# Attention and a two-layer network on one core: part of the early pooling on GpSimd, and seven products in a sixth chunk's second layer

## The chip, the cores and the metric

The kernel runs on one core of one Trainium2 chip. The core has five engines that the program feeds: TensorE (PE; its weight loads are shown apart as PEld), VectorE (DVE), ScalarE (ACT), GpSimd (POOL) and SyncE (SP, which here only starts transfers), and 16 DMA engines. Each engine takes its instructions in the order in which the program gives them and waits at the first one that isn't ready. The metric is the device time of one execution in microseconds (us); of several runs the median is given.

## The reference, cut to what matters

```python
# q, k, v: (8, 8, 576, 64)      moe_x is the attention's output as (8, 576, 512)
k_p = k.reshape(B, H, 72, 8, D).mean(axis=3)         # keys and values pooled by 8
v_p = v.reshape(B, H, 72, 8, D).mean(axis=3)
scores = (1/8) * q @ k_p.T;  scores -= max(scores)
attn = exp(scores) / (sum(exp(scores)) + 1e-9)
x = attn @ v_p                                       # 4608 tokens of 512
xn = (x - mean(x)) / sqrt(var(x) + 1e-6) * g_ln
out = x + maximum(xn @ w_ch1, 0) @ w_ch2             # 512 -> 2048 -> 512
```

## The kernel before, in words

**Numbers.** Results have to be good to float32, while TensorE is fed 16-bit numbers. So each large factor is kept as a high part and a low part, both float16, and each product is three matmuls (high by high, high by low, low by high). Wherever a factor is made, two steps make it: one rounds to the high part (mostly on ScalarE), one subtracts to get the low part (VectorE or GpSimd).

**Tiles and chunks.** The 4608 tokens are 36 tiles of 128; four tiles make a chunk of 512 (nine chunks, 0 to 8). For each batch of 576 tokens the keys and values are pooled first. `load_k`/`pool_k` (L622 to L630) load four pairs of heads of 128x72x8 numbers; a reduce on VectorE (L627) sums the innermost eight, and two copies (L630) put the halves on the diagonal blocks of `kblk`. `load_v`/`pool_v` (L634 to L640) do it for each of eight heads (72x64x8), with one reduce into `vp` (L640). When a batch's `vp` is whole, `max_v` takes its largest value (L644) and `all_max` spreads it over the partitions with a small matmul (L447), after which `split_v` makes the scaled high and low parts `vh`, `vb`, and a DMA lays `vh` out as `va` for the matmuls. Batch 0's values and keys are pooled by functions of their own.

`stage_a` of a tile is scores, maximum and exponentials (matmuls L754); `stage_b` is the values (matmuls L886, L887), the division, the mean and variance, and the normalized `z` with its two parts. Where a tile holds tokens of two batches, L893 copies two batches' scales into `cvm`. From chunk 3 on, L935 makes the normalization's bias from mean and scale (`ln`), one number for each of 128 tokens, for ScalarE.

**The network.** Chunks 0 and 1 have plain products in layer 1 (`ffn_in`, matmuls L1070); from chunk 2 on layer 1 is done as a 2x2 scheme with seven products in place of eight (`product`, L1114). In layer 2, chunks 0 to 3 have plain products (`ffn_out`, matmuls L1265: eight groups of 24 matmuls of 512 columns for a chunk, each group with one accumulation into `x`, L1276). Chunks 4 to 8 have seven products (`out_seven`, L1231: 336 matmuls of 256 columns for a chunk, with 28 groups of 12). `C_TWO = 4` is the first of these. Plain and seven-product chunks prepare the hidden activations differently: `whole_h` (ScalarE L1140, VectorE L1144) for the plain ones; for seven products `left_factors`, `right_relu`, `right_sums` and `right_pair`: a rounding on ScalarE and the low part (L1152) on VectorE or GpSimd, with four sums on GpSimd in between (L1169, L1170, L1172, L1173). `right_pair` with i = 1 always takes its low part on GpSimd, with i = 0 only for chunks in `LO_GPSIMD`. Seven products also need seven factors of w2. Four of them are sums that `sums_w2` makes once (tokens TW; VectorE, GpSimd, ScalarE) and writes to DRAM (`w2s`); three are copies (KW); each chunk loads its factors again, in 14 transfers of 512 KB (`load_w2`, L1220), into four buffers that lie in the place of `ring`.

**The order.** Two tables, START and STEADY, set the order of all work. A token names a function and its arguments; each time it stands in the table, that function runs on by one step (to its next `yield`), so that the tables interleave matmuls, splits, loads and prepared batches. All engines' queues, the DMA queue of SP among them, follow from this one order. START reaches up to the first `product`; the weights w1 and w2 are also loaded, taken to float32 (`convert`, tokens C, L520) and split in it (`split`, tokens S: L460 or L462 the high part on ScalarE, L467 the low part on VectorE, or L464 on GpSimd for the four blocks of w2's first half that `LO_POOL` names; the first second-layer matmuls, tokens G.0, need them), so that it holds work for VectorE, ScalarE and GpSimd that later stretches don't.

Of the kernel before, what the change touches and what calls it, by code (L numbers as in the profile page):

```python
# [31 lines left out]
C_TWO = 4  # L32
# [33 lines left out]
R.2.1 R.2.1 A.3 D.0 D.0 R.2.2 R.2.2 A.3 M1.0 B.1 A.3 A.3 E.3.0 M1.0 M1.0 S.1.0 E.3.0 B.1 B.1 B.0 B.0 B.0 E.2.0 E.2.0
E.2.1 E.2.1 B.2 E.3.1 B.1 C.2.0 S.1.0 S.1.0 S.1.1 C.2.0 C.2.0 C.1.3 C.1.3 C.1.2 C.1.2 S.1.1 S.1.1 B.2 B.2 B.0 B.0 B.1
S.1.2 E.3.1 B.2 E.3.0 E.3.0 S.1.2 S.1.2 S.1.3 C.2.2 C.2.1 E.3.1 E.3.1 B.3 HK.1.1 HK.1.1 R.2.3 R.2.3 A.4 R.1.4 R.1.4 B.1
B.1 HK.1.1 HK.1.1 A.4 A.5 S.1.3 S.1.3 F.0.0.0 F.0.1.0 F.0.0.0 B.2 F.0.1.0 A.4 A.5 F.0.2.0 A.4 F.0.2.0 C.2.2 HV.1.0
HV.1.0 F.0.0.0 F.0.0.0 F.0.3.0 F.0.3.0 C.2.3 F.0.1.0 F.0.1.0 F.0.4.0 F.0.4.0 C.2.2 C.2.2 C.2.1 C.2.1 C.2.1 HV.1.0  # L70
# [287 lines left out]
def attn_ffn_kernel(ctx: ExitStack, tc: tile.TileContext, qT, kT, v, kvn, kvt, g, w1, w2, out):  # L358
# [264 lines left out]

    def pool_k(b, p):
        kr = kraw.pop((b, p))
        kp = kr.rearrange("p k l -> p (k l)")[:, 0:KV]
        nc.vector.tensor_reduce(out=kp, in_=kr, axis=AX.X, op=ALU.add)  # L627
        for j in range(2):
            r, c = slice(j * D, (j + 1) * D), slice(j * KV, (j + 1) * KV)
# [776 lines left out]
```

## Time and profile before

| | us |
|---|---|
| median of 3 runs | 821.44 (820.87 to 822.48) |
| the profiled execution: its own time | 825.36 |
| its span | 823.6 |
| mean granted TensorE clock | 0.990 |

| busy in the span | us | share | instructions |
|---|---|---|---|
| PE | 788.5 | 96% | 6462 |
| DVE | 655.3 | 80% | 1328 |
| ACT | 453.5 | 55% | 848 |
| POOL | 441.4 | 54% | 521 |

The span is from the first to the last event of the profiled execution; 1.8 us of its time lie around it. A view by windows gives the busy time of each engine in each stretch, with the number of instructions, the granted clock of TensorE (1.00 is full speed), and the share of the 16 DMA engines' time. A view of waits says for how long an engine stood and which event ended it. Rows of a group of instructions have the line, the engine, the operation, out and in, the shape, the count, then the busy time in us, the mean of one in ns, and the idle time of the engine just before them with what ended it. The chain of waits is followed back from the last instruction.

### The profile page before, as it was taken

Reading aid. Unit: us, or ns where it says so; the run is one execution under the profiler, and the core shown is the slowest. Engines: PE = TensorE matmul, PEld = TensorE weight load, DVE = VectorE, ACT = ScalarE, POOL = GpSimd, SP = SyncE. Lnnn points to the kernel's source line nnn. Section 1 sums busy time; section 2 is a strip of 40 time slices with the busy share of each in tenths; the row PEclk is TensorE's granted clock in tenths of the full one; section 3 lists DMA queues with packets and bytes.
Section 4 is the critical chain, followed back from the end, with each engine's and each line's share of the span. In section 5 each row is a group of like instructions: output and inputs, shape, how many; then the busy total and the mean of one; then the engine's idle time right before and its main releaser. Section 6 shows DMA issues by size and latency. Waiting matters only on the chain.

```text
span 823.6 us, 16934 instructions
## 1 busy us (share of the span) xinstructions
PE 788.5 (96%) x6462; PEld 595.7 (72%) x6462; DVE 655.3 (80%) x1328; ACT 453.5 (55%) x848; POOL 441.4 (54%) x521
## 2 busy tenths in 40 slices
PE   6988999899999999999999999999999999999997
PEld 3876445444448765775668899889988889988886
DVE  5998999689586989789868988889788768765653
ACT  3988794141315635454448374856575737655461
POOL 0535335345261515763437574577488757785473
PEclk9989999899999999999999999999999999999999
DMA  9949746631045777666537469686756663654224
GB/s 359 333 125 254 215 126 141 150 90 27 1 106 146 168 157 185 164 158 153 134 105 205 155 190 221 152 243 137 214 146 156 174 178 99 166 166 142 90 104 153
DMA packets 179201, 131.54 MB, mean 160 GB/s; under 512 B 143536, under 2 KB 150832, under 8 KB 176944
## 3 DMA queue, kind: packets, MB, share of 16 engines
q1 hardware_dynamic: 177968, 129.57, 58.3%
q10 hardware_dynamic: 1152, 0.90, 0.5%
q8 instruction: 50, 0.82, 0.4%
q14 instruction: 31, 0.25, 0.1%
HBM read 81.79 MB, written 16.78 MB: 120 GB/s over the span
## 4 chain that ended last, share of the span: by engine, by line
PE 75%; DVE 16%; DMA 2%; ACT 2%; POOL 2%; issue 2%; ACTq 1%; DVEq 0%; POOLq 0%
PE ps_f L1114 29%; PE ps_f L1231 19%; PE ps_f L1265 13%; PE ps_f L1070 7%; PE ps_a L754 4%; DVE w L520 2%; DVE w L467 1%; PE ps_a L886 1%; DVE x L1248 1%; PE ps_m L694 1%; PE ps_a L887 1%; DMA vr<-in_v_dram 1%; DVE x L1276 1%; DVE raw L595 1%; DVE wm L504 1%
## 5 line engine op out<-in xcount | busy, mean ns | idle before, releaser
L1114 PE MATMUL ps_f<-zts,w 128*128 128x256 f16 x1680 | 207.2, 273 | 0.9 <-DVE x L1276 0.8
L1231 PE MATMUL ps_f<-ring,w 128*128 128x256 f16 x1680 | 193.7, 273 | 3.8 <-DVE x L1248 2.8
L1231 PEld LDWEIGHTS <-w 128*128 128x128 f16 x1680 | 163.7, 98 | 24.4 <-issue 4.0
L1114 PEld LDWEIGHTS <-w 128*128 128x128 f16 x1680 | 163.4, 98 | 22.1 <-issue 1.5
L1265 PE MATMUL ps_f<-w,ring 128*128 128x512 f16 x768 | 170.0, 379 | 1.5 <-DVE ring L1144 1.4
L1265 PEld LDWEIGHTS <-ring 128*128 128x128 f16 x768 | 74.2, 98 | 88.9 <-DVE ring L1144 3.6
L1133 ACT COPY raw<-ps_f 128x256 f32<-128x256 f32 x168 | 59.1, 372 | 94.3 <-PE ps_f L1114 87.5
L1152 POOL TENSOR_TENSOR w<-w 128x512 f16<-128x512 f32 x64 | 75.1, 1177 | 35.7 <-ACT w L1150 28.4
L1114 PE MATMUL ps_f<-zts,tsp 128*128 128x256 f16 x672 | 91.1, 273 | 0.8 <-ACT raw L1133 0.8
L1070 PE MATMUL ps_f<-zts,w 128*128 128x512 f16 (+1 forms) x480 | 88.4, 343 | 2.5 <-DVE x L1276 1.6
L790 POOL TENSOR_TENSOR phl<-e,phl 128x512 f16<-128x512 f32 x32 | 38.6, 1206 | 73.2 <-ACT phl L780 73.1
L1070 PEld LDWEIGHTS <-w 128*128 128x128 f16 x480 | 47.2, 99 | 40.4 <-issue 6.8
L1150 ACT CAST w<-w 128x512 f16<-128x512 f32 x80 | 48.9, 619 | 46.0 <-POOL w L1170 17.9
L1114 PEld LDWEIGHTS <-tsp 128*128 128x128 f16 x672 | 65.2, 98 | 9.4 <-issue 1.1
L1039 POOL TENSOR_TENSOR hl<-raw,hl 128x640 f16<-128x640 f32 x28 | 40.3, 1444 | 31.6 <-ACT hl L1037 23.2
L1248 DVE SCALAR_TENSOR_TENSOR x<-ps_f,y,x 128x256 f32<-128x256 f32 (+1 forms) x70 | 35.4, 518 | 26.2 <-PE ps_f L1231 25.6
L1248 DVE SCALAR_TENSOR_TENSOR x<-ps_f,cy,x 128x256 f32<-128x256 f32 (+1 forms) x70 | 35.2, 516 | 17.3 <-PE ps_f L1231 16.8
L1128 DVE TENSOR_TENSOR raw<-ps_f,raw 128x256 f32<-128x256 f32 x84 | 34.0, 416 | 18.5 <-PE ps_f L1114 9.6
L754 PE MATMUL ps_a<-kblk,q 128*128 128x144 f32 (+1 forms) x320 | 41.9, 289 | 1.7 <-issue 1.2
L754 PEld LDWEIGHTS ps_a<-kblk,q 128*128 128x128 f32 (+1 forms) x320 | 37.0, 179 | 4.9 <-issue 2.4
L1039 POOL TENSOR_TENSOR hl<-z,hl 128x512 f16<-128x512 f32 x18 | 23.9, 1327 | 30.8 <-ACT hl L1037 16.5
L1079 ACT ACTIVATE ring<-ps_f 128x512 f16<-128x512 f32 (+1 forms) x40 | 19.5, 508 | 37.9 <-PE ps_f L1070 33.3
(175 smaller groups left out, 1416.0 us busy)
## 6 DMA issues: line engine op xcount, KB each, us to landing
ring<-w2s SPq DMA_DIRECT2D x70, 512.0 KB
q<-in_qT_dram SPq DMA_DIRECT2D x36, 256.0 KB
out_dram<-x SPq DMA_DIRECT2D x36, 256.0 KB
tsp<-in_w_dram SPq DMA_DIRECT2D x8, 1024.0 KB
kr<-in_kT_dram SPq DMA_DIRECT2D x28, 288.0 KB
vr<-in_v_dram SPq DMA_DIRECT2D x56, 144.0 KB
raw<-in_w_dram SPq DMA_DIRECT2D x6, 1024.0 KB
w2s<-phl SPq DMA_DIRECT2D x32, 128.0 KB
```

The source lines that it names most:

```text
L754: nc.tensor.matmul(ps[r, p // 2, p % 2 * 2 * KV : (p % 2 + 1) * 2 * KV], lhsT=q[:, p, r], rhs=kblk[b % NKB][:, p, :], start=True, stop=True,)
L790: nc.gpsimd.tensor_tensor(out=ph[:, 0, :, KA:P], in0=e[:, :, 0:KA], in1=ph[:, 0, :, 0:KA], op=ALU.subtract)
L1039: nc.gpsimd.tensor_tensor(out=zhl[:, 1, :], in0=src, in1=zhl[:, 0, :], op=ALU.subtract)
L1070: nc.tensor.matmul(ps, lhsT=w[:, part, fs], rhs=zT[:, kz, cols], start=(n == 0), stop=(n == 3 * NKT - 1),)
L1114: nc.tensor.matmul(ps, lhsT=w[:, part, f * P : (f + 1) * P], rhs=z, start=m in (1, 2, 4, 5) and n == 0, stop=m in (2, 3, 4, 7) and n == 3 ...
L1128: nc.vector.tensor_tensor(out=o, in0=ps, in1=o, op=ALU.add)
L1133: nc.scalar.copy(out=o, in_=ps)
L1150: nc.scalar.copy(out=hi, in_=src)
L1152: engine.tensor_tensor(out=lo, in0=src, in1=hi, op=ALU.subtract)
L1231: nc.tensor.matmul(ps, lhsT=wt[2][:, left, part, f * HC + u * P : f * HC + (u + 1) * P], rhs=b[:, f // FPB, wp, f % FPB], start=n < 4 and ...
L1248: nc.vector.scalar_tensor_tensor(out=x, in0=ps, scalar=scale, in1=x, op0=ALU.mult, op1=ALU.add)
L1265: nc.tensor.matmul(ps, lhsT=h[:, part, i, cols], rhs=w[:, wp, j], start=(n == 0), stop=(n == 3 * NFT // 2 - 1),)
```

## The change

- `C_TWO` is 3, and STEADY has chunk 3's second layer as seven products (`out_seven` with its four preparing functions and its 14 loads) in place of eight groups of plain products and `whole_h`.
- `V_GPSIMD = (1, 2)`: the values of batches 1 and 2 (16 heads) are pooled by GpSimd, in three additions that halve each time (72x256, 72x128, 72x64), from a host layout in which the eight tokens of a group are not innermost. `K_GPSIMD = (2,)`: the same for the four key pairs of batch 2 (128x288, 128x144, then two additions of 64x72 that write straight to `kblk` and take the place of the two copies).
- `LO_GPSIMD` is empty: the low parts of `right_pair` with i = 0 in chunks 6, 7 and 8 (24 subtractions of 128x512) go from GpSimd to VectorE.
- The copies of L893 (eight of 64x3) go from VectorE to ScalarE. The bias of L935 (24 of 128x1) is written as a `tensor_scalar` with two scalars in place of a `scalar_tensor_tensor`. The place of `z` is taken one step later.
- START and STEADY are new tables: nearly all tokens stand elsewhere.

The counts that differ, by the kind of instruction (lines of the kernel before; left before, right with the change):

| engine, work | before | changed |
|---|---|---|
| PE L1265, matmul of 512 columns | 768 | 576 |
| PE L1231, matmul of 256 columns | 1680 | 2016 |
| DVE L640, reduce of one head's values | 56 | 40 |
| DVE L627, reduce of one pair's keys | 28 | 24 |
| DVE L630, copy into `kblk` | 56 | 48 |
| DVE L1144 / ACT L1140 | 32 | 16 |
| DVE L1276 | 32 | 24 |
| DVE L1248 (128x256 / 128x512) | 120 / 20 | 144 / 24 |
| DVE L1152, low part of 256 / of 512 from `raw`, `phl` | 40 / 40 | 48 / 48 |
| L1152, low part of 512 from `w`: DVE / POOL | 16 / 64 | 48 / 48 |
| POOL L1169, L1170, L1172, L1173, each | 40 | 48 |
| POOL, additions for pooling | 0 | 64 |
| SP, loads of 512 KB from `w2s` | 70 | 84 |

Three places show what the new order moves. In the changed program the line numbers are larger: L464 is L483 there, L790 and L793 are L823 and L826, L520 is L539, L640 and the new additions are L670 to L673, L1081 is L1114, L894 to L915 are L927 to L948, L1210 is L1243, L1220 is L1253.

GpSimd's queue around the four low parts of w2's first half (L464, `w` of 128x1024), before:

```order
L789 MEMSET phl_116 128x8x40
L790 TENSOR_TENSOR phl_116<-e,phl_116 128x8x64
L793 TENSOR_TENSOR phl_116<-e,phl_116 128x8x8
L464 TENSOR_TENSOR w_91<-w_91 128x1024
L790 TENSOR_TENSOR phl_115<-e,phl_115 128x8x64
L793 TENSOR_TENSOR phl_115<-e,phl_115 128x8x8
L719 MEMSET vh 72x8
L720 MEMSET vb 72x8
L464 TENSOR_TENSOR w_91<-w_91 128x1024 x3
L926 COPY ln<-cvm 128x2
```

and now:

```order
L483 TENSOR_TENSOR w_91<-w_91 128x1024
L647 TENSOR_TENSOR kr<-kr 128x288
L648 TENSOR_TENSOR kr<-kr 128x144
L655 TENSOR_TENSOR kblk_113<-kr 64x72 x2
L483 TENSOR_TENSOR w_91<-w_91 128x1024
L823 TENSOR_TENSOR phl_115<-e,phl_115 128x8x64
L826 TENSOR_TENSOR phl_115<-e,phl_115 128x8x8
L483 TENSOR_TENSOR w_91<-w_91 128x1024
L671 TENSOR_TENSOR vr<-vr 72x256
L672 TENSOR_TENSOR vr<-vr 72x128
L673 TENSOR_TENSOR vp<-vr 72x64
L483 TENSOR_TENSOR w_91<-w_91 128x1024
```

Before, three of the four stand in a row, with two attention tiles' low parts (`phl`) ahead. Now a pair of keys (L647 to L655) stands between the first and the second and a head of values (L671 to L673) ahead of the fourth; the eight heads of batch 1 stand further ahead in the queue.

VectorE's queue where w2 is taken to float32 (L520 before, L539 now), layer 1 of chunk 0 is taken out of PSUM (L1081 before, L1114 now) and a tile's values are finished, before:

```order
L640 TENSOR_REDUCE vp<-vr 72x64
L1081 SCALAR_TENSOR_TENSOR ring<-ps_f,ring 128x256 x2
L520 SCALAR_TENSOR_TENSOR w_91<-w_91,raw 128x1024
L640 TENSOR_REDUCE vp<-vr 72x64
L1081 SCALAR_TENSOR_TENSOR ring<-ps_f,ring 128x256
L894 TENSOR_SCALAR sm<-ps_a,cv 128x8
L902 RECIPROCAL rs<-sm 128x8
L904 TENSOR_TENSOR x<-ps_a,rs 128x512
L914 BN_STATS st<-x 128x6
L915 BN_AGGR ln<-st 128x2
L1081 SCALAR_TENSOR_TENSOR ring<-ps_f,ring 128x256 x2
L640 TENSOR_REDUCE vp<-vr 72x64
```

and now:

```order
L1114 SCALAR_TENSOR_TENSOR ring<-ps_f,ring 128x256
L539 SCALAR_TENSOR_TENSOR w_91<-w_91,tsp_92 128x1024
L539 SCALAR_TENSOR_TENSOR w_91<-w_91,tsp_93 128x1024
L927 TENSOR_SCALAR sm<-ps_a,cv 128x8
L935 RECIPROCAL rs<-sm 128x8
L937 TENSOR_TENSOR x<-ps_a,rs 128x512
L947 BN_STATS st<-x 128x6
L948 BN_AGGR ln<-st 128x2
L1114 SCALAR_TENSOR_TENSOR ring<-ps_f,ring 128x256 x2
L797 TENSOR_REDUCE mx<-ps_a 128x8
L802 TENSOR_TENSOR e<-ps_a,mx 128x576
L1114 SCALAR_TENSOR_TENSOR ring<-ps_f,ring 128x256
```

The reduces of single heads (L640) that stood between these are gone from VectorE's queue; two steps of w2 stand next to each other and the next tile's maximum and exponent step (L797, L802) follows sooner.

SP's queue around the first load of a w2 factor for the seven products (`ring<-w2s`), with the last writes of the sums to `w2s` ahead of it, before:

```order
L1210 DMA w2s_122<-phl_116 128x4x128 x2
L1281 DMA out_dram<-x 128x512
L634 DMA vr<-in_v_dram 72x512
L622 DMA kr<-in_kT_dram 128x576
L1281 DMA out_dram<-x 128x512
L634 DMA vr<-in_v_dram 72x512
L1220 DMA ring<-w2s_121 128x2048
L746 DMA q<-in_qT_dram 128x512
L634 DMA vr<-in_v_dram 72x512
L1281 DMA out_dram<-x 128x512
L801 DMA_TRANSPOSE pt<-phl_115 128x16x128
L1220 DMA ring<-w2s_121 128x2048
```

and now:

```order
L1243 DMA w2s_122<-phl_116 128x4x128 x4
L1314 DMA out_dram<-x 128x512
L661 DMA vr<-in_v_dram 72x512
L641 DMA kr<-in_kT_dram 128x576
L1243 DMA w2s_122<-phl_116 128x4x128 x2
L1253 DMA ring<-w2s_121 128x2048
L779 DMA q<-in_qT_dram 128x512
L661 DMA vr<-in_v_dram 72x512
L1253 DMA ring<-w2s_121 128x2048
L1314 DMA out_dram<-x 128x512
L834 DMA_TRANSPOSE pt<-phl_115 128x16x128
L661 DMA vr<-in_v_dram 72x512
```

Before, the first of these loads is the 178th row of SP's queue and comes for chunk 4; now it is the 152nd and comes for chunk 3, close behind the last write of the sums.

The diff, without the tables' rows:

```diff
-C_TWO = 4
+C_TWO = 3
...
-LO_GPSIMD = (6,7,8)
+K_GPSIMD, V_GPSIMD = (2,), (1, 2)
+LO_GPSIMD = ()
 START = """
-LN.2 LN.2 LK.0 LK.0 LK.1 LK.1 Q.0 Q.0 HK.1.0 R.1.0 R.1.0 V0 V0 K0 K0 K0 HK.1.0 HK.1.0 Q.1 Q.1 R.1.1 R.1.1 R.1.2 R.1.2
...
+LN.2 LN.2 LK.0 LK.0 LK.1 LK.1 Q.0 Q.0 R.1.0 R.1.0 R.1.1 R.1.1 Q.1 Q.1 R.1.2 R.1.2 R.1.3 R.1.3 A.0 HV.1.0 LG LG R.2.0
...
 def pool_k(b, p):
         kr = kraw.pop((b, p))
-        kp = kr.rearrange("p k l -> p (k l)")[:, 0:KV]
-        nc.vector.tensor_reduce(out=kp, in_=kr, axis=AX.X, op=ALU.add)
+        if b in K_GPSIMD:
+            kr = kr.rearrange("p k l -> p (k l)").rearrange("p (l k) -> p l k", k=KV)
+            nc.gpsimd.tensor_add(out=kr[:, 0:4, :], in0=kr[:, 0:4, :], in1=kr[:, 4:8, :])
+            nc.gpsimd.tensor_add(out=kr[:, 0:2, :], in0=kr[:, 0:2, :], in1=kr[:, 2:4, :])
+        else:
+            kp = kr.rearrange("p k l -> p (k l)")[:, 0:KV]
+            nc.vector.tensor_reduce(out=kp, in_=kr, axis=AX.X, op=ALU.add)
         for j in range(2):
...
-            nc.vector.tensor_copy(out=kblk[b % NKB][r, p, c], in_=kp[r])
+            if b in K_GPSIMD:
+                nc.gpsimd.tensor_add(out=kblk[b % NKB][r, p, c], in0=kr[r, 0, :], in1=kr[r, 1, :])
+            else:
+                nc.vector.tensor_copy(out=kblk[b % NKB][r, p, c], in_=kp[r])
...
-        nc.vector.tensor_reduce(out=vp[b][:, h, :], in_=vr, axis=AX.X, op=ALU.add)
+        if b not in V_GPSIMD:
+            nc.vector.tensor_reduce(out=vp[b][:, h, :], in_=vr, axis=AX.X, op=ALU.add)
+            return
+        vr = vr.rearrange("p d l -> p (d l)").rearrange("p (l d) -> p l d", d=D)
+        nc.gpsimd.tensor_add(out=vr[:, 0:4, :], in0=vr[:, 0:4, :], in1=vr[:, 4:8, :])
+        nc.gpsimd.tensor_add(out=vr[:, 0:2, :], in0=vr[:, 0:2, :], in1=vr[:, 2:4, :])
+        nc.gpsimd.tensor_add(out=vp[b][:, h, :], in0=vr[:, 0, :], in1=vr[:, 1, :])
...
-                nc.vector.tensor_copy(out=cv[r], in_=CV[b][r])
+                nc.scalar.copy(out=cv[r], in_=CV[b][r])
...
         if c > 2:
-            nc.vector.scalar_tensor_tensor(
-                out=ln[:, 0:1], in0=ln[:, 0:1], scalar=-1.0, in1=ln[:, 2:3], op0=ALU.mult, op1=ALU.mult
+            nc.vector.tensor_scalar(
+                out=ln[:, 0:1], in0=ln[:, 0:1], scalar1=ln[:, 2:3], scalar2=-1.0, op0=ALU.mult, op1=ALU.mult
             )
...
```

More of the change, by code (lines that the diff above doesn't have):

```diff
@@ L66 @@
[L66 to L70, printed above, removed]
@@ L101 @@
+F.1.15 F.1.15 V.10 HV.3.1 F.1.13 F.1.13 F.1.14 F.1.14 F.1.15 F.1.15 G.1.0.1 G.1.1.1 G.1.2.1 HK.3.1 HK.3.1 B.8 B.8 V.10
+U.1.1 U.1.0 V.10 V.10 HV.3.1 V.10 V.10 X X U.1.0 U.1.0 B.11 B.11 G.1.0.1 G.1.3.1 G.1.1.1 B.11 B.11 HV.3.1 HV.3.1 B.11
+B.11 B.11 G.1.0.1 G.1.0.1 HK.3.1 HK.3.1 U.0.0 U.0.0 U.1.1 U.1.1 G.1.2.1 G.1.2.1 G.1.2.1 G.1.1.1 G.1.1.1 G.1.3.1 G.1.3.1
+G.1.3.1
 """
 STEADY = """
-P.2.0.1.2 P.2.0.0.2 P.2.0.0.5 P.2.0.1.1 P.2.0.1.5 P.2.0.0.1 P.2.0.1.1 P.2.0.1.1 HV.4.0 A.12 A.12 A.13 TW.0.0.0 TW.0.0.0
@@ new lines @@
+P.4.1.0.7 A.22 P.4.1.0.5 P.4.1.0.5 P.4.1.0.3 P.4.0.3.3 P.4.0.3.3 EL.4.0.3 P.4.1.0.4 P.4.1.0.4 P.4.0.3.4 P.4.0.3.4
+EP.4.0.1.1 EP.4.0.1.0 EP.4.0.1.0 B.21 A.23 A.22 EL.4.0.3 EL.4.0.3 O.4.0.1.1 ES.4.0.2 EP.4.0.2.0 P.4.0.3.7 P.4.0.3.7
+O.4.0.1.0 ER.4.0.3 P.4.1.0.7 P.4.1.0.7 P.4.1.1.5 P.4.1.1.1 EP.4.0.1.1 EP.4.0.1.1 P.4.1.0.3 P.4.1.0.3 O.4.0.0.1
+O.4.0.0.0 EP.4.0.2.0 EP.4.0.2.0 ER.4.0.3 ER.4.0.3 ES.4.0.2 ES.4.0.2 B.20 B.20 EP.4.0.2.1 HV.6.1 HV.6.1 A.22 A.22
+LW.4.0.3 LW.4.0.3 ER.4.0.2 ER.4.0.2 P.4.1.1.5 P.4.1.1.5 EL.4.1.0 B.20 P.4.1.1.3 ES.4.0.3 EP.4.0.3.0 A.23 B.22 A.23
@@ new lines @@
+HV.6.1 HV.6.1 P.4.1.2.5 P.4.1.2.5 O.4.0.5.0 O.4.0.5.0 P.4.1.3.2 P.4.1.2.6 P.4.1.3.6 P.4.1.3.5 P.4.1.2.3 B.23 P.4.1.3.6
+P.4.1.3.6 P.4.1.2.6 P.4.1.2.6 P.4.1.3.5 P.4.1.3.5 B.22 B.22 P.4.1.2.2 P.4.1.2.2 P.4.1.2.4 P.4.1.3.7 P.4.1.3.3
+EP.4.1.0.1 EP.4.1.0.1 P.4.1.3.2 P.4.1.3.2 P.4.1.3.4 P.4.1.2.7 ES.4.1.1 ES.4.1.1 EP.4.1.1.1 Z.22.0 HV.6.1 P.4.1.2.3
+P.4.1.2.3 EL.4.1.2 P.4.1.2.4 P.4.1.2.4 Z.22.1 P.4.1.3.4 P.4.1.3.4 EP.4.1.1.0 EP.4.1.1.0 Z.22.0 Z.22.0 B.23 A.24
+EL.4.1.2 EL.4.1.2 Z.22.1 Z.22.1 P.4.1.3.3 P.4.1.3.3 EL.4.1.3 P.4.1.3.7 P.4.1.3.7 P.4.1.2.7 P.4.1.2.7 ER.4.1.2
@@ L353 @@
+O.8.1.5.0 O.8.1.5.1 O.8.1.5.1 O.8.1.5.1
 """
@@ L916, in values @@
         seven = c >= 2
-        if seven and tt >= 2:
-            if "z" not in t_raw:
-                t_raw["z"] = t_raw["b"].rearrange("p n c -> p (n c)")
-            z = t_raw["z"][:, :DM]
-        else:
+        Z[t] = ln
+        if not (seven and tt >= 2):
             z = wk1.tile([P, DM], F32, name="z")
-        Z[t] = ln
         if not seven:
@@ L933, in values @@
             yield
+            if tt >= 2:
+                if "z" not in t_raw:
+                    t_raw["z"] = t_raw["b"].rearrange("p n c -> p (n c)")
+                z = t_raw["z"][:, :DM]
         if c > 2:
-            nc.vector.scalar_tensor_tensor(
-                out=ln[:, 0:1], in0=ln[:, 0:1], scalar=-1.0, in1=ln[:, 2:3], op0=ALU.mult, op1=ALU.mult
+            nc.vector.tensor_scalar(
+                out=ln[:, 0:1], in0=ln[:, 0:1], scalar1=ln[:, 2:3], scalar2=-1.0, op0=ALU.mult, op1=ALU.mult
             )
@@ L1386 @@
         "qT": q.transpose(1, 3, 0, 2).reshape(NPAIR, P, NTT, P).transpose(2, 1, 0, 3),
-        "kT": k.reshape(B, NPAIR, 2, KV, POOL, D).transpose(0, 2, 5, 1, 3, 4).reshape(B, P, NPAIR, KV, POOL),
-        "v": v.reshape(B, H, KV, POOL, D).transpose(0, 2, 1, 4, 3),
+        "kT": np.stack([
+            k[i].reshape(NPAIR, 2, KV, POOL, D).transpose((1, 4, 0, 3, 2) if i in K_GPSIMD else (1, 4, 0, 2, 3)).reshape(P, NPAIR, KV, POOL)
+            for i in range(B)
+        ]),
+        "v": np.stack([
+            v[i].reshape(H, KV, POOL, D).transpose((1, 0, 2, 3) if i in V_GPSIMD else (1, 0, 3, 2)).reshape(KV, H, D, POOL)
+            for i in range(B)
+        ]),
         "kvn": np.stack([x[i].transpose(1, 0, 2).reshape(S, DM)[: S // P * P].reshape(S // P, P, DM).transpose(1, 0, 2) for x, i in ((k, 1), (v, 1), (v, 0))]),
```

573 lines of the change are left out of this document (291 added, 282 removed).

## The prediction, made before the changed kernel was run

> **What bounds the kernel now.** I read first the busy time of the engines, then the windows, then TensorE's waits in the windows where it stands, then the groups of those windows. The sum is made against the profiled execution: 825.36 us, of which the span is 823.6 and 1.8 lie around it. It is 3.9 above the median of the runs (821.44); the change is worked out in the span and then taken off the median.
>
> ```profile
> span 823.6 us, 16934 instructions
> PE 788.5 (96%) x6462; PEld 595.7 (72%) x6462; DVE 655.3 (80%) x1328; ACT 453.5 (55%) x848; POOL 441.4 (54%) x521
> ```
>
> TensorE works for 96% of the span and is idle for 35.1 us. So there are two ways to be faster: less work for TensorE, or fewer of these 35 us. The windows (start and end, length, then the busy time of each engine) show where they lie:
>
> ```profile
> core 0: us, PE busy (x) PEld busy (x) DVE busy (x) ACT busy (x) POOL busy (x), PEclk, DMA share, GB/s
> 0.00:20.60 20.60, 13.48 (x61) 7.72 (x61) 11.93 (x30) 6.34 (x8) 2.03 (x12) 1.00 0.92 359
> 20.60:103.00 82.40, 72.30 (x633) 55.25 (x634) 76.75 (x153) 69.65 (x98) 36.24 (x34) 0.96 0.76 232
> 103.00:144.10 41.10, 41.06 (x228) 20.74 (x226) 39.94 (x68) 29.07 (x41) 17.91 (x14) 1.00 0.54 133
> 144.10:164.70 20.60, 18.02 (x98) 8.32 (x97) 14.23 (x35) 3.25 (x5) 6.23 (x12) 0.83 0.69 150
> 164.70:245.90 81.20, 78.74 (x380) 35.80 (x379) 65.27 (x106) 21.79 (x38) 39.50 (x39) 1.00 0.22 55
> 245.90:448.00 202.10, 199.48 (x1589) 141.36 (x1589) 167.78 (x369) 105.10 (x214) 95.10 (x136) 1.00 0.64 154
> 448.00:597.00 149.00, 146.64 (x1399) 131.51 (x1398) 127.26 (x270) 90.00 (x181) 89.88 (x105) 1.00 0.73 191
> 597.00:803.00 206.00, 203.80 (x1950) 181.80 (x1948) 145.22 (x290) 126.14 (x263) 146.81 (x165) 1.00 0.51 142
> ```
>
> From 245.9, where START ends, TensorE is busy for 99% of each window up to 803: a matmul removed there comes off the end, as long as no other engine becomes late. START, in contrast, leaves 7.1 + 10.1 + 0.0 + 2.6 + 2.5 = 22.3 us idle, and VectorE is busy for 93% and 97% of the windows from 20.6 to 144.1. What ended TensorE's longest waits in START (total, times, longest):
>
> ```profile
> PE ps_m L694 <- DMA w<-in_kvn_dram: 6.2, 1, 6.2
> PE ps_m L835 <- ACT w L460: 4.5, 1, 4.5
> PE ps_m L447 <- DVE rowmax L425: 3.7, 2, 2.0
> PE ps_a L886 <- DMA va<-vh: 2.6, 1, 2.6
> ```
>
> The first is the first load, the second ScalarE. The third is a spread of a maximum that VectorE, late in its queue, hadn't given, and the fourth the layout `va` of a batch's values, a transfer behind eight heads' pooling and the maximum. Only the last two hang on the pooling.
>
> **The change part by part. 1: chunk 3's second layer.** Two pieces of the chain of waits (start, duration, work) hold unbroken matmuls of both kinds:
>
> ```profile
> 224.33 20.73 PE ps_f L1265 x96
> 799.63 18.36 PE ps_f L1231 x168
> ```
>
> A matmul of 512 columns takes 20.73/96 = 0.2159 us, one of 256 columns 18.36/168 = 0.1093. 192 of the first (41.45) go and 336 of the second (36.72) come: **-4.7 us** of TensorE's work. The order shows exactly these counts, so this term is the surest; it needs the preparation (part 3) to be in time.
>
> **2: the pooling.** What leaves VectorE, and what GpSimd has that is nearest to its new additions:
>
> ```profile
> L640 DVE TENSOR_REDUCE vp<-vr x56: 646/673/683, 30.5 to 538.0; 72x64 f32<-72x512 f32 x56
> L627 DVE TENSOR_REDUCE kr<-kr 128x72 f32<-128x576 f32 x28 | 20.8, 742 | 0.1
> L630 DVE COPY kblk<-kr 64x72 f32<-64x72 f32 x20 | 9.9, 496 | 0.5
> L1169 POOL TENSOR_TENSOR w<-raw 128x256 f32<-128x256 f32 x26 | 21.2, 814 | 34.0 <-ACT raw L1161 32.6 <-DVE w L1152 0.9
> L1201 POOL TENSOR_TENSOR kr<-kr 128x128 f32<-128x128 f32 x16 | 8.5, 531 | 0.5
> L793 POOL TENSOR_TENSOR phl<-e,phl 128x64 f16<-128x64 f32 x32 | 13.7, 428 | 0.0
> ```
>
> (The copies' row is that of the window 20.6 to 245.9.) VectorE loses 16 x 0.673 + 4 x 0.742 + 8 x 0.496 = 17.7 us, all in START. GpSimd gets 16 x (0.814 + 0.531 + 0.428) = 28.4 for the values; for the keys, by the same rows with the elements' share added, 4 x (0.9 + 0.56 + 2 x 0.44) = 9.4 (estimates): 37.8 in all. GpSimd's windows to 245.9 hold 101.9 us of work, so there is room.
>
> But GpSimd's work isn't free for VectorE. The copies of L630 show it, and a pair of rows of the same window (both 128x512; the longer of them is the one whose engine was last released by GpSimd):
>
> ```profile
> L630 DVE COPY kblk<-kr x56: 190/195/1441, 12.7 to 605.8; 64x72 f32<-64x72 f32 x56
> L595 DVE TENSOR_TENSOR raw<-w 128x512 f32<-128x512 f16 x16 | 13.5, 899 | 1.0 <-POOL w L583 1.0
> L599 DVE TENSOR_TENSOR raw<-raw 128x512 f32<-128x512 f32 x4 | 2.7, 677 | 0.1
> ```
>
> A copy that takes 190 ns alone takes up to 1441, while L640 keeps to 646 to 683 whatever runs beside it. In START the copies lose 20 x (496 - 190) = 6.1 us and L595 16 x (899 - 677) = 3.6, 9.7 us for 101.9 of GpSimd's work; 37.8 more would cost VectorE 3.6, call it 4. Here a rule speaks against the change. The Trainium skill, "SBUF — State Buffer", section "Who interferes with whom", says that the port pair shared by VectorE and GpSimd is an exclusive lock, taken by copies in a two-port mode and by operations with two inputs in that memory, while a reduce on trn2 never contends. The trace agrees on the reduces (646 to 683) and the copies (190 to 1441). By the rule the change removes what never contends and adds what holds the lock, and in the worst case all of the 17.7 us is given back: rival A below.
>
> What START gains lies between two ends. At most the waits named go: 3.7 + 2.6 us, and the slow matmuls after the second of them:
>
> ```profile
> 126.94 2.59 PE ps_f L1070 x12
> 150.90 4.50 DMA va<-vh
> 156.75 5.12 PE ps_f L1070 x12
> ```
>
> The same twelve matmuls take 5.12 in place of 2.59 after the idle time, with the granted clock at 0.83 in that window: 2.5 more, 8.8 in all. The other end is a stall: GpSimd's queue now holds nine heads (9 x 1.77 = 16) and a pair of keys (2.3), 18.3 us, ahead of the fourth low part of w2's first half, which before ran at once:
>
> ```profile
> L464 POOL TENSOR_TENSOR w<-w x4: 2129/2134/2139, 69.3 to 85.2; 128x1024 f16<-128x1024 f32 x4
> ```
>
> Ahead of 85.2 GpSimd was idle for about half of the time, which covers the additions if their loads come in time; if not, L464, the two attention low parts behind it and the first matmuls of G.0 stand (up to 18.3 less what remains of cover). I take **-6**: two thirds of the 8.8, since of 17.7 us some 4 are lost again; ends -14 (below, rival C) and +9.
>
> **3: what chunk 3 asks of the other engines.** Rows for what goes and comes:
>
> ```profile
> L1144 DVE SCALAR_TENSOR_TENSOR ring<-raw,ring 128x512 f16<-128x512 f32 x32 | 23.6, 781 | 2.1 <-ACT ring L1140 2.0
> L1276 DVE SCALAR_TENSOR_TENSOR x<-ps_f,cy,x 128x512 f32<-128x512 f32 x28 | 20.7, 742 | 2.6 <-PE ps_f L1265 2.1
> L1248 DVE SCALAR_TENSOR_TENSOR x<-ps_f,y,x 128x256 f32<-128x256 f32 (+1 forms) x70 | 35.4, 518 | 26.2 <-PE ps_f L1231 25.6
> L1152 DVE TENSOR_TENSOR w<-raw,w 128x256 f16<-128x256 f32 (+1 forms) x52 | 34.4, 667 | 4.9 <-ACT w L1150 4.9
> L1152 DVE TENSOR_TENSOR w<-w 128x512 f16<-128x512 f32 x16 | 13.7, 858 | 0.3 <-ACT w L1150 0.3
> L1152 POOL TENSOR_TENSOR w<-w 128x512 f16<-128x512 f32 x64 | 75.1, 1177 | 35.7 <-ACT w L1150 28.4 <-PE ps_f L1231 5.1 <-DVE x L1248 2.1
> ```
>
> VectorE: -16 x 0.781 - 8 x 0.742 + 28 x 0.518 + 16 x 0.667 + 8 x 0.858 = +13.6. GpSimd: 8 x 4 sums at about 0.8 plus 8 x 1.177 = +35. Both fall into 245.9 to 448, as do the sums of w2, which must now be in DRAM for a load that is the 152nd of SP's queue, not the 178th. VectorE there has 34 us free and GpSimd 107; VectorE would go from 83% to about 92%. Ends: -1 and +7 (the window 20.6 to 103, with VectorE at 93%, leaves TensorE 12% idle; on some 60 us that is 7). I take **+1**: the load comes early, but at 83% this window lost only 2.6 in 202. The 14 more loads of 512 KB add 7 MB to windows with the DMA engines at 64%; hidden.
>
> **4: the small edits.** 24 low parts go to VectorE in chunks 6 to 8 (24 x 0.858 = +20.6, GpSimd -28.2): in 597 to 803 VectorE is at 145 of 206 us, so its own free time hides them; uncovered, a subtraction that is late for L1231 costs its 0.86. Ends -1 (GpSimd's 1.177 is the slower) and +2; I take 0. The next two rows
>
> ```profile
> L893 DVE COPY cvm<-cv 64x3 f32<-64x3 f32 x8 | 3.9, 484 | 0.1
> L935 DVE SCALAR_TENSOR_TENSOR ln<-ln 128x1 f32<-128x1 f32 x24 | 8.5, 353 | 0.6 <-POOL ln L926 0.5
> ```
>
> give VectorE at most 3.9 + 8.5 us back over the whole span, mostly where TensorE has no wait: 0.
>
> **Sum:** -4.7 - 6 + 1 + 0 = **-9.7**. The profiled execution would be 815.7 and its span 813.9; from the median, 821.44 - 9.7 = **811.7 us**.
>
> **The rivals.** *A: only TensorE's work shrinks.* VectorE waits for the port, or the waits go elsewhere in START, and START is as long as before: 821.44 - 4.7 = 816.7. For it: L630's 1441 ns, and ScalarE at 69.65 of 82.4 us, which isn't relieved. Against: L640's 17.7 us are a fifth of VectorE's work in the two fullest windows.
> *B: slower, GpSimd's queue bounds START.* In-order GpSimd waits at additions for heads whose loads come late (the DMA engines are at 76% there), and the fourth L464 stands behind. It decides from the point at which loads eat GpSimd's free half ahead of 85 us. Half of the 18.3 us exposed is +9, less 4.7: 821.44 + 4.3 = 825.7. For it: nine heads ahead, one queue. Against: heads were loaded by 30.5 for the first reduce already.
> *C: START loses nearly all of its waits.* A new order could hide all but the first load (6.2) and L835 (4.5): 22.3 - 10.7 + 2.5 = 14.1, with -4.7 in all -18.8: 802.6. Against it: it takes 7.8 us out of waits that the named rows don't explain by pooling or VectorE.
> *D: the stretch to 448 turns VectorE-bound:* +7 in place of +1: 817.7.
>
> **How the numbers follow.** The forecast has 0.48, with its own range 806 to 815.5; A 0.20, B 0.10, C 0.12, D 0.10. The range 803 to 821 leaves out B and half of C. A change within 0.2% (1.6 us) is what a measurement of this kernel can't tell from none: 819.8 to 823.1. Faster: the forecast, C, most of A and of D, 0.82; slower: B, 0.10; same 0.08, from the upper edges of A and D.
>
> **What would show it.** Right: L1231 with 2016 matmuls and TensorE's work lower by 4 to 6 us in the middle; START's idle time of TensorE down from 22.3 to about 16, no wait for `va`, 0.83 gone from the granted clock; VectorE's busy share in START lower. Wrong: a wait of L1298 (the plain second layer) for GpSimd's L483 means B; VectorE's remaining operations longer by 10 us or more, A; waits of L1264 for VectorE before 450, D. If the low parts of chunks 6 to 8 appear as waits of TensorE after 597, part 4 was wrong.

## The result, and the profile after

The changed kernel takes **830.08 us** (median of 4 runs, 828.41 to 830.3), where the kernel before has 821.15: a ratio of 1.010 (95% interval 1.008 to 1.012). It is slower by 8.9 us; 811.7 was forecast, and the range ended at 821. The profiled execution took 830.30 us, its span 828.6.

```profile
span 828.6 us, 17360 instructions
PE 786.4 (95%) x6606; PEld 610.3 (74%) x6606; DVE 662.2 (80%) x1344; ACT 472.2 (57%) x888; POOL 491.4 (59%) x601
```

TensorE has 2.1 us less work than before (788.5) and 7.1 us more idle time (42.2 for 35.1). The 336 matmuls that replace 192 are there (6606 in all), so 4.7 us were saved; 2.6 of them came back as slower matmuls, as will be seen. Windows of START, in the columns of before:

```profile
0.00:20.60 20.60, 13.41 (x61) 7.57 (x61) 11.65 (x26) 8.30 (x11) 1.85 (x10) 1.00 0.92 358
20.60:103.00 82.40, 69.40 (x601) 53.26 (x602) 69.43 (x138) 65.28 (x94) 61.11 (x80) 0.92 0.71 225
103.00:144.10 41.10, 38.56 (x222) 19.68 (x219) 39.02 (x63) 29.53 (x40) 31.91 (x35) 1.00 0.71 151
```

In the second window VectorE is less busy (69.4 for 76.8 us), as the change meant, and yet TensorE did less there (601 matmuls for 633) and at a granted clock of 0.92 (before 0.96). An engine that has been relieved and doesn't get further is waiting. The waits of VectorE, longest sums first (total, times, longest):

```profile
DVE x L1281 <- PE ps_f L1264: 35.5, 43, 2.8
DVE sm L927 <- ACT cvm L926: 16.7, 4, 6.4
DVE ring L1114 <- ACT ring L1112: 12.8, 12, 1.9
```

The first is VectorE waiting for TensorE, which costs nothing. The second did not exist before: in four places VectorE stood for 16.7 us until ScalarE had made `cvm`, the copies of 64x3 numbers that the change took off VectorE. The copy itself is nothing; the first of them, in ScalarE's timeline (start, duration), comes behind all of this:

```profile
86.00 1.14 ACT L531 ACTIVATE w<-tsp 128x1024 f32<-128x1024 f32 x1
87.02 1.16 ACT L535 ACTIVATE tsp<-tsp 128x1024 int32<-128x1024 uint16 x1
88.04 1.16 ACT L531 ACTIVATE w<-tsp 128x1024 f32<-128x1024 f32 x1
89.08 1.14 ACT L535 ACTIVATE tsp<-tsp 128x1024 int32<-128x1024 uint16 x1
90.09 0.69 ACT L811 ACTIVATE e<-e 128x576 f32<-128x576 f32 x1
90.81 1.04 ACT L813 CAST phl<-e 128x1024 f16<-128x1024 f32 x1
91.77 0.29 ACT L816 CAST phl<-e 128x128 f16<-128x128 f32 x1
91.96 0.39 ACT L926 COPY cvm<-cv 64x3 f32<-64x3 f32 x2
```

Nothing of this work is needed for the tile whose values are being finished; it only stands ahead in the order. VectorE's and TensorE's rows (the bracket: idle before, and what ended it) show what follows:

```profile
92.39 0.23 DVE L927 TENSOR_SCALAR sm<-ps_a,cvm 128x8 f32<-128x8 f32 x1 [6.42 <-ACT cvm L926]
92.88 0.69 DVE L937 TENSOR_TENSOR x<-ps_a,rs 128x512 f32<-128x512 f32 x1
93.72 0.21 PE L919 MATMUL ps_a<-va,pt 128*128 128x65 f16 x1 [3.64 <-DVE x L937]
94.88 4.43 PE L1298 MATMUL ps_f<-w,ring 128*128 128x512 f16 x10
```

VectorE is idle for 6.42 us; the tile's place in PSUM, where TensorE leaves its results, stays taken until L937 has read it, so TensorE's next values wait 3.64 us; and after the idle time its matmuls run at 443 ns in place of 216 for a while (4.43 us for 10: 2.3 more). VectorE is held up in the same way at 282.7 (4.00 us idle), 469.6 (3.65) and 653.1 (2.66), together 16.7; how much of each reaches TensorE differs. Before, the copies were on VectorE, right ahead of L894, which then waited for TensorE alone.

### The profile page after: what moved, and what is told of

It is laid out like the page before. It is cut to its first block, busy times and chain, and to the rows that moved or that the text cites. A ratio compares the mean times of both kernels' runs of the same rounds, so it can differ in the third digit from the quotient of the medians.

```text
span 828.6 us, 17360 instructions
## 1 busy us (share of the span) xinstructions
PE 786.4 (95%) x6606; PEld 610.3 (74%) x6606; DVE 662.2 (80%) x1344; ACT 472.2 (57%) x888; POOL 491.4 (59%) x601
## 4 chain that ended last, share of the span: by engine, by line
PE 49%; DVE 9%; ACT 2%; DMA 1%; issue 1%; POOL 1%; DVEq 0%; POOLq 0%; ACTq 0%
PE ps_f L1147 23%; PE ps_f L1264 22%; DVE w L1185 2%; PE ps_a L787 2%; PE ps_f L1298 1%; DVE x L1281 1%; DMA pt<-phl 1%; DMA ring<-w2s 1%; ACT w L1183 1%; DVE ring L1177 1%; PE ps_a L919 1%; PE ps_a L920 0%; DVE raw L1161 0%; ACT raw L1189 0%; DVE phl L1161 0%
## 5 line engine op out<-in xcount | busy, mean ns | idle before, releaser
L1264 PE MATMUL ps_f<-ring,w 128*128 128x256 f16 x2016 | 233.4, 273 | 5.2 <-DVE x L1281 3.0
L1264 PEld LDWEIGHTS <-w 128*128 128x128 f16 x2016 | 197.0, 98 | 30.8 <-issue 4.0
L1147 PEld LDWEIGHTS <-w 128*128 128x128 f16 x1680 | 163.5, 98 | 25.3 <-issue 5.8
L1298 PE MATMUL ps_f<-w,ring 128*128 128x512 f16 x576 | 129.1, 384 | 3.0 <-DVE x L1309 2.2
L1298 PEld LDWEIGHTS <-ring 128*128 128x128 f16 x576 | 56.7, 99 | 71.4 <-issue 7.2
L1183 ACT CAST w<-w 128x512 f16<-128x512 f32 x96 | 59.1, 619 | 43.9 <-POOL w L1203 23.9
L1185 POOL TENSOR_TENSOR w<-w 128x512 f16<-128x512 f32 x48 | 59.0, 1228 | 30.9 <-ACT w L1183 23.1
L1103 PEld LDWEIGHTS <-w 128*128 128x128 f16 x480 | 46.5, 98 | 37.6 <-issue 2.1
L823 POOL TENSOR_TENSOR phl<-e,phl 128x512 f16<-128x512 f32 x32 | 39.4, 1232 | 44.0 <-ACT phl L813 37.7
L1202 POOL TENSOR_TENSOR w<-raw 128x256 f32<-128x256 f32 x32 | 24.7, 771 | 68.1 <-ACT raw L1194 37.8
L1281 DVE SCALAR_TENSOR_TENSOR x<-ps_f,y,x 128x256 f32<-128x256 f32 (+1 forms) x84 | 42.0, 517 | 22.7 <-PE ps_f L1264 21.6
L1281 DVE SCALAR_TENSOR_TENSOR x<-ps_f,cy,x 128x256 f32<-128x256 f32 (+1 forms) x84 | 42.1, 517 | 14.4 <-PE ps_f L1264 13.9
L1185 DVE TENSOR_TENSOR w<-raw,w 128x512 f16<-128x512 f32 (+1 forms) x64 | 45.0, 710 | 3.9 <-ACT w L1183 3.9
```

Of the source, the lines that this page charges most:

```text
L823: nc.gpsimd.tensor_tensor(out=ph[:, 0, :, KA:P], in0=e[:, :, 0:KA], in1=ph[:, 0, :, 0:KA], op=ALU.subtract)
L1103: nc.tensor.matmul(ps, lhsT=w[:, part, fs], rhs=zT[:, kz, cols], start=(n == 0), stop=(n == 3 * NKT - 1),)
L1147: nc.tensor.matmul(ps, lhsT=w[:, part, f * P : (f + 1) * P], rhs=z, start=m in (1, 2, 4, 5) and n == 0, stop=m in (2, 3, 4, 7) and n == 3 ...
L1183: nc.scalar.copy(out=hi, in_=src)
L1185: engine.tensor_tensor(out=lo, in0=src, in1=hi, op=ALU.subtract)
L1264: nc.tensor.matmul(ps, lhsT=wt[2][:, left, part, f * HC + u * P : f * HC + (u + 1) * P], rhs=b[:, f // FPB, wp, f % FPB], start=n < 4 and ...
```

## The experiments

All kernels were timed beside the kernel before on the same chip; ratios are against it, and "us" in the table is the ratio less 1, times 823.7, the median of before in these runs; it can differ by up to 1.5 us from the difference of two medians. Beside the change itself before had 821.15, 2.5 us less, so a distance between the change and another row is known to about 3 us only. The changed kernel's START and STEADY tables hold all of the work of their part, so that either can be combined with the other part of before.

| run | START order | pooling of b = 1, 2 | STEADY | `cvm` copies | ratio (95%) | us |
|---|---|---|---|---|---|---|
| the change | new | GpSimd | new | ScalarE | 1.010 (1.008 to 1.012) | +8.2 |
| start_whole | new | GpSimd | old | ScalarE | 1.0099 (1.0073 to 1.0125) | +8.2 |
| start_order | new | VectorE | old | ScalarE | 1.0308 (1.0277 to 1.0339) | +25.4 |
| pool_only | old | GpSimd | old | ScalarE | 1.0228 (1.0196 to 1.0260) | +18.8 |
| steady_only | old | VectorE | new | ScalarE | 1.0093 (1.0066 to 1.0119) | +7.7 |
| before_cvm | old | VectorE | old | ScalarE | 1.0089 (1.0065 to 1.0113) | +7.3 |
| after_cvm | new | GpSimd | new | VectorE | 0.9897 (0.9872 to 0.9922) | -8.5 |
| start_whole_cvm | new | GpSimd | old | VectorE | 0.9969 (0.9952 to 0.9986) | -2.6 |
| steady_cvm | old | VectorE | new | VectorE | 0.9925 (0.9897 to 0.9953) | -6.2 |
| pool_only_cvm | old | GpSimd | old | VectorE | 1.0134 (1.0115 to 1.0153) | +11.0 |
| after_early | new | GpSimd | new | ScalarE, a step earlier | 0.9920 (0.9905 to 0.9935) | -6.6 |
| after_cvm_lo | new | GpSimd | new, low parts of chunks 6 to 8 on GpSimd | VectorE | 0.9973 (0.9959 to 0.9986) | -2.2 |
| before_ln | old | VectorE | old | VectorE | 0.9979 (0.9964 to 0.9995) | -1.7 |

Apart from before_cvm and before_ln, which are the kernel before with one edit, all of these have L935 in its new form and the later place of `z`, which no run tries alone.

### The change taken apart

The first four runs cut it at the end of START and separate the order from the pooling. Their edits, start_order's here, are of this kind (for the old tables, the rows of before stand in place of the new ones):

```diff
-C_TWO = 3
+C_TWO = 4
...
-K_GPSIMD, V_GPSIMD = (2,), (1, 2)
-LO_GPSIMD = ()
+K_GPSIMD, V_GPSIMD = (), ()
+LO_GPSIMD = (6,7,8)
...
 STEADY = """
-P.2.0.0.2 P.2.0.0.1 P.2.0.0.5 P.2.0.1.2 P.2.0.0.1 P.2.0.0.1 P.2.0.0.6 P.2.0.1.1 P.2.0.1.1 P.2.0.1.1 P.2.0.0.5 P.2.0.0.5
+P.2.0.1.2 P.2.0.0.2 P.2.0.0.5 P.2.0.1.1 P.2.0.1.5 P.2.0.0.1 P.2.0.1.1 P.2.0.1.1 HV.4.0 A.12 A.12 A.13 TW.0.0.0 TW.0.0.0
...
```

> The changed START alone: its table and the pooling on GpSimd, with the two small edits, in front of the old STEADY (chunk 3 plain, low parts of chunks 6 to 8 on GpSimd). The two traces put START's end at 248.1 us in place of 245.9. If the loss of 8.9 us sits in START (theory S), this is +5 to +9 against the kernel before; if it sits behind START (theory T), it is +1 to +3; by the forecast it was -6.

> As start_whole, but all pooling back on VectorE; the new START table stays. If GpSimd's additions hold up VectorE and GpSimd's own queue (theory port), START is shorter without them: 2 to 6 us below start_whole. If the table is what costs (theory order), VectorE, which gets 17.7 us back, makes it worse: 5 to 15 above start_whole.

> The kernel before with both old tables, and only the pooling moved to GpSimd (and the two small edits). Theory port: the 44 us or so of GpSimd's work cost as much as they relieve, 0 to +6 against before. If the relief works as forecast, -3 to -8.

> The old START with the pooling on VectorE, in front of the changed STEADY (seven products in chunk 3, low parts of chunks 6 to 8 on VectorE), with the two small edits. By the sum of matmuls -4.7 and by the forecast -3.7; if the loss sits behind START (theory T: the trace has 6.3 us more of TensorE's idle time from 263 to 350), +2 to +7.

Measured: +8.2, +25.4, +18.8 and +7.7. The two halves of the change each cost as much as the whole. That doesn't fit a loss that sits in one half, nor two losses that add up; it points to what both have in common, the small edits that were left in. Both traces have VectorE's wait for `cvm` in four places (15.3 and 16.0 us). Neither theory S nor T of these expectations holds.

### The copies

The second four take back one edit, or make it alone:

```diff
-                nc.scalar.copy(out=cv[r], in_=CV[b][r])
+                nc.vector.tensor_copy(out=cv[r], in_=CV[b][r])
```

> The changed kernel with one edit undone: the eight copies into cvm are on VectorE again. Theory copy: on ScalarE they wait behind work that was queued earlier, VectorE stands for them (16.7 us in four places) and TensorE behind it (3.64 + 2.5 at half clock near 94 us, about 3 near 285, some 2 to 4 to 337, 3.5 near 473): 8 to 13 below the changed kernel, 817 to 822 on the scale where it has 830.1 and the kernel before 821.2. If the new order and GpSimd's additions cost by themselves, less than 3 is won back.

> The kernel before with that one edit alone: the eight copies into cvm on ScalarE. Theory copy: +5 to +12 against the kernel before, with VectorE waiting for ScalarE ahead of a value tile in four places. If the copies are harmless: within 1 us.

> start_whole (changed START with the pooling on GpSimd, old STEADY) with the copies back on VectorE. Theory copy: -6 to -1 against the kernel before, where start_whole had +8.2. If the changed START costs by itself, +3 or more stay.

> steady_only (old START, changed STEADY with seven products in chunk 3) with the copies back on VectorE. Theory copy: -5 to -1 against the kernel before (the sum of matmuls alone is -4.7), where steady_only had +8.4. If chunk 3 overloads the stretch before it, it stays above +2.

In the kernel before, this edit alone, in the other direction, costs +7.3 us (before_cvm). Its VectorE waits:

```profile
DVE sm L894 <- ACT cvm L893: 14.6, 4, 5.7
```

In the changed kernel, taking it back wins 2.0% by the ratios (1.010 to 0.9897), 16.7 us; the medians are 13.8 us apart (830.08 to 816.32) and the two profiled spans 13.7 (828.6 to 814.9). Either is more than expected, and after_cvm is faster than both kernels: 816.32 us (815.51 to 817.84). Both halves turn from slower to faster, to -2.6 and -6.2. So the copies are the cause of the whole loss. They cost the changed kernel about twice what they cost the kernel before (13.7 to 16.7 us against 5.2 in the trace and 7.3 by the ratio). By the traces (after_cvm and the change, at the same matmul of the same program) the change loses 4.7 us up to the end of START, 2.5 more to 350 us, 5.0 from there to 480 and 1.5 behind: 13.7, of which TensorE's idle time is 10.0 and the rest slower matmuls. Before_cvm's trace has 5.2 us more idle time than that of before. Why the new order covers less of it was not tried.

### Position or engine

Does a hand-over to ScalarE cost, or the place in its order? In after_early the copies stay on ScalarE but are issued ahead of the tile's matmuls:

```diff
             cv = scalar_tile("cvm", 3)
+            for r, b in segs:
+                nc.scalar.copy(out=cv[r], in_=CV[b][r])
...
-        if len(segs) > 1:
-            for r, b in segs:
-                nc.scalar.copy(out=cv[r], in_=CV[b][r])
```

> The changed kernel with the copies into cvm still on ScalarE, but issued ahead of the tile's value matmuls, one step of its function earlier. Theory queue position: what costs is that the copies stand in ScalarE's order behind work that VectorE doesn't need yet, so that the early copies cost nothing: as after_cvm, 1.0% below the kernel before, and no wait of VectorE's sm for them. If it is ScalarE's handing over that costs, or any copy there, it stays near the changed kernel, 1.0% above.

0.9920: the loss is gone, and the intervals of after_early and after_cvm overlap. The copies take as long as before (the row with its shortest, median and longest), and VectorE's four `sm` that use them (L926 in this kernel) don't wait for them any more:

```profile
L906 ACT COPY cvm<-cv x8: 177/189/190, 80.5 to 635.6; 64x3 f32<-64x3 f32 x8
L926 DVE TENSOR_SCALAR sm<-ps_a,cvm x4: 210/215/217, 85.5 to 638.9; 128x8 f32<-128x8 f32 x4
```

It is the place in the order, not the engine. The Trainium skill, "PSUM — Partial Sum Buffer", section "Engine vs sequencer instructions", says that the queues of ScalarE, VectorE and GpSimd are strict first-in first-out; the trace agrees, with a 0.19 us copy for which VectorE stood 6.42 us.

### The pooling and the other small edits

> Both old tables and only the pooling on GpSimd (the copies into cvm on VectorE). pool_only, with the copies on ScalarE, stood 18.9 us above before, of which the copies explain some 8.5. Theory order: GpSimd's additions pay only in an order that is made for them, so +6 to +12 stay. If the pooling by itself was worth the forecast 6 us, -3 to -8.

Both tables old, only the additions on GpSimd: +11.0. The relief of VectorE is worth less than nothing in an order that wasn't made for it. START ends at 255.5 us in its trace (before: 245.9), so the loss sits there. TensorE's longest waits show why: the keys' `kblk` comes late from GpSimd, a wait that before doesn't have, and the spread of the maxima, which follow the pooling, has 8.0 us for 3.7. The middle row is the first load, 6.2 before:

```profile
PE ps_m L448 <- DVE rowmax L426: 8.0, 4, 2.6
PE ps_m L709 <- DMA w<-in_kvn_dram: 6.5, 1, 6.5
PE ps_a L769 <- POOL kblk L637: 5.0, 1, 5.0
```

Together with start_order, the new order with the pooling on VectorE (+25.4, where start_whole has +8.2), it says that order and pooling are one edit: the pooling alone costs 11.0, the new order without it stands 17.2 above the same order with it, and both together win 2.6.

> after_cvm with the 24 low parts of chunks 6 to 8 back on GpSimd. The forecast cost this part at 0 (ends -1 and +2): the same as after_cvm within 2 us. If the low parts on VectorE were worth something, 2 to 6 above after_cvm.

```diff
-LO_GPSIMD = ()
+LO_GPSIMD = (6,7,8)
```

821.32 us for after_cvm's 816.32 (0.9973 for 0.9897): in this order the low parts on VectorE are worth 5 to 6 us. After_cvm_lo's trace loses 3.7 us between the 1344th matmul of `product` (555.3 us; 557.1 in after_cvm) and the last, and TensorE waits there for GpSimd, which in after_cvm it never does:

```profile
PE ps_f L1264 <- POOL w L1185: 1.2, 1, 1.2
```

> The kernel before with L935 alone as a tensor_scalar with two scalars. The forecast was 0: within 1.6 us of before. In the traces it takes 204 ns (196 to 214) in place of 160 (142 to 1107).

0.9979, -1.7 us, at the edge of what can be told from nothing.

## Why the prediction was wrong, by its own steps

**The step that failed is part 4**, the sentence on L893 and L935: they "give VectorE at most 3.9 + 8.5 us back over the whole span, mostly where TensorE has no wait: 0". It costed what the copies take on VectorE, and nothing of what they wait for on ScalarE. The change adds a wait, of L927 for ScalarE, and the prediction didn't name what stands ahead of the copy in ScalarE's order (4 us of w1 conversions), nor what stands behind L927 on VectorE (all of its work) and who waits for that (TensorE's next values, through PSUM). Worth: 13.7 to 16.7 us in the changed kernel, 7.3 alone. The rows for it were there: ScalarE at 69.65 of 82.4 us in the second window was quoted, but for another purpose. With this one term set right, the total stands: after_cvm's ratio of 0.9897 (0.9872 to 0.9922) holds the 0.988 of the forecast. But that is in part luck. Its parts, below, are other than forecast: START and chunk 3 gave less than their terms, and two terms that were put at nothing, the low parts and L935, made up for it.

**Part 1, chunk 3's second layer (-4.7), and part 3 (+1).** TensorE's work shrank as forecast: 788.5 us before, 783.8 in steady_cvm. Steady_cvm's -6.2 (-8.5 to -3.9), however, holds more than the -3.7 of these two parts: L935 with its -1.7, and the low parts of chunks 6 to 8. Its trace beside that of before_ln, which has the same START table and the same L935, shows what was won where. The first row of each goes from the end of START to the 1344th matmul of `product`, by when chunk 3 is finished, the second from there to the end (before_ln, then steady_cvm):

```profile
244.00:560.60 316.60, 312.50 (x2668) 242.29 (x2668) 264.26 (x577) 176.12 (x358) 166.32 (x218) 1.00 0.65 165
560.60:820.90 260.30, 252.58 (x2403) 225.63 (x2400) 179.80 (x364) 147.43 (x303) 171.97 (x194) 0.99 0.56 152
```

```profile
244.00:559.30 315.30, 309.06 (x2812) 257.05 (x2812) 278.83 (x607) 192.17 (x389) 202.29 (x261) 0.99 0.73 186
559.30:817.30 258.00, 252.56 (x2403) 225.49 (x2400) 187.06 (x389) 148.40 (x304) 144.32 (x171) 1.00 0.56 155
```

Chunk 3's stretch is 1.3 us shorter: TensorE works 3.4 us less there and is idle for 2.1 more, where +1 was taken. With the new START the same stretch takes 313.7 (after_cvm), 315.0 (after_early) and 315.2 us (after_cvm_lo), so 1.3 to 2.9 were won of the 3.7. The wait that was feared showed, small, in after_cvm's trace, where chunk 3's seven products begin at 362.6 us; all of the first two rows and 0.6 us of the third come before that:

```profile
PE ps_f L1298 <- DVE x L1309: 2.2, 1, 2.2
PE ps_f L1147 <- ACT raw L1166: 1.7, 2, 1.1
PE ps_f L1147 <- DVE raw L1161: 1.4, 2, 0.8
```

**Part 2, START (-6): the term mis-sized.** Start_whole_cvm has -2.6 (-4.0 to -1.2), L935's -1.7 in it, so that START alone is hardly told from nothing by the times. The traces have the sign: START ends at 245.9, 244.0 and 244.0 us with the old table and the pooling on VectorE (before, before_ln, steady_cvm), at 243.0, 243.4, 242.4 and 240.1 with the new one (start_whole_cvm, after_cvm, after_early, after_cvm_lo), 2.4 us less in the mean. Up to START's end, before and then start_whole_cvm:

```profile
0.00:245.90 245.90, 223.59 (x1395) 127.83 (x1396) 208.10 (x388) 130.10 (x188) 101.91 (x109) 0.97 0.55 161
0.00:243.00 243.00, 223.10 (x1395) 127.64 (x1396) 200.06 (x360) 130.10 (x188) 143.25 (x173) 0.98 0.57 165
```

TensorE's idle time went from 22.3 to 19.9 us, not to 16. The waits that were to go went: in after_cvm's START the one for `va` is gone and the spread of maxima has 0.6 of 3.7 us. Others took their place:

```profile
PE ps_m L868 <- ACT w L479: 6.2, 2, 4.7
PE ps_a L787 <- issue: 2.5, 2, 1.3
PE ps_f L1103 <- DVE w L486: 1.4, 1, 1.4
```

ScalarE, which nothing relieves, has 6.2 for 4.5 (4.0 in after_cvm_lo's trace), and VectorE is late once more. Two prices were too low. GpSimd's additions in after_cvm (window 20.6 to 245.9):

```profile
L671 POOL TENSOR_TENSOR vr<-vr 72x256 f32<-72x256 f32 x16 | 15.4, 962 | 1.9 <-DMA vr<-in_v_dram 1.7
L672 POOL TENSOR_TENSOR vr<-vr 72x128 f32<-72x128 f32 x16 | 11.6, 725 | 1.3
L673 POOL TENSOR_TENSOR vp<-vr 72x64 f32<-72x64 f32 x16 | 8.5, 532 | 1.3
```

The values take 35.5 us, not 28.4, and with the keys it is 45.5, not 37.8. And VectorE, which was to lose 17.7 us and to get 4 of them back, is busy for only 8.0 us less by the two rows above: some 10 came back (about 8 when each instruction is counted for itself, as the sum did), near the 10 that the prediction named as a sign of rival A. That goes with the additions, not with the order: in the new order VectorE has 206.1 us up to START's end with the pooling on it (start_order) and 199.5 with the pooling on GpSimd (start_whole), 6.6 less. Some of VectorE's operations with two inputs became longer, in after_cvm:

```profile
L614 DVE TENSOR_TENSOR raw<-w 128x512 f32<-128x512 f16 x16 | 15.1, 1003 | 0.0
L486 DVE SCALAR_TENSOR_TENSOR w<-w,gs 128x1024 f16<-128x1024 f32 x8 | 13.7, 1713 | 0.0
L539 DVE SCALAR_TENSOR_TENSOR w<-w,tsp 128x1024 int32<-128x1024 int32 x7 | 9.4, 1354 | 0.0
L539 DVE SCALAR_TENSOR_TENSOR w<-w,raw 128x1024 int32<-128x1024 int32 x6 | 9.1, 1533 | 0.0
```

Before, in the same window, they had means of 899, 1389, 1217 and 1214 ns: 16 x 104 + 8 x 324 + 7 x 137 + 6 x 319 = 7.1 us for these four groups. Start_order, with the new order and the pooling on VectorE, tells what of it belongs to the additions:

```profile
L597 DVE TENSOR_TENSOR raw<-w 128x512 f32<-128x512 f16 x16 | 16.2, 1071 | 0.0
L469 DVE SCALAR_TENSOR_TENSOR w<-w,gs 128x1024 f16<-128x1024 f32 x8 | 11.1, 1382 | 0.1
L522 DVE SCALAR_TENSOR_TENSOR w<-w,tsp 128x1024 int32<-128x1024 int32 x7 | 8.6, 1244 | 0.0
L522 DVE SCALAR_TENSOR_TENSOR w<-w,raw 128x1024 int32<-128x1024 int32 x6 | 7.2, 1220 | 0.0
```

The first group is as long without the additions; its 1.7 us come with the order. The other three are near their old means, so 5.3 us of after_cvm's (8 x 331 + 7 x 110 + 6 x 313) come with the additions, for three groups alone, where 4 was taken for all. The port rule that the prediction drew on (the Trainium skill, "SBUF — State Buffer", section "Who interferes with whom") is borne out in direction by these three; START's gain ended more than halfway to rival A. Against A the prediction also read a row too high: the 17.7 us are 15% of VectorE's 116.7 us in the two fullest windows, not a fifth.

**The low parts of chunks 6 to 8 (0).** Against the kernel before no run isolates them, but behind the 1344th matmul of `product`, where they lie, the traces with the new table and the low parts on VectorE have 258.0, 257.8 and 258.3 us (steady_cvm, after_cvm, after_early), those with the old table 260.3 and 261.4 (before_ln, start_whole_cvm), and after_cvm_lo, the new table with them on GpSimd, 261.7. Some 2 to 3 us were won where 0 stood, beyond the end of -1, and only with the low parts on VectorE.

**The rivals.** B, the slower one, forecast 825.7 and had the sign, but not the cause: the fourth low part of w2's first half started at 86.6 us, where before it started at 85.2, and TensorE waits nowhere for it. A's mechanism is part of what shrank START's gain. C didn't come, and of D only the waits above.

## What to carry to other kernels

A tiny operation that is moved to an engine with free time takes that engine's place in the order, not its free time: look at what stands ahead of it there at the moment when it's needed, and who waits behind the one that needs it. Where an operand is known early, issue the copy early; then the other engine is as good. An edit that is costed at its duration alone, beside a large one that is worked out with care, is the one to test by itself first.

## What the runs showed of the hardware that was not expected

The bias of L935 as a `tensor_scalar`, with one tensor input and two scalars, hardly varies, where the two-input form took up to 1107 ns (shortest, median, longest; the change first, then the kernel before; before_ln, with this edit alone, has 197, 204 and 214):

```profile
L968 DVE TENSOR_SCALAR ln<-ln x24: 196/204/214, 269.9 to 729.9; 128x1 f32<-128x1 f32 x24
```

```profile
L935 DVE SCALAR_TENSOR_TENSOR ln<-ln x24: 142/160/1107, 267.8 to 726.0; 128x1 f32<-128x1 f32 x24
```

Its median is longer (204 for 160 ns), and its mean shorter (204 for 353). START's own end moves between executions of the same START: the first matmul of `product` comes at 243.4 us in after_cvm's profiled execution and at 240.1 in after_cvm_lo's, whose instructions up to there are the same. A term of 2 or 3 us in START can't be read from one trace.
